# Three passes over the experts' weights: token operands of passes 2 and 3 made in pass 1, roundings one product later, weight differences beside the raw weights

## The chip, the cores and the metric

The kernel runs on one core of one Trainium2 chip. The metric is the device time of one execution in microseconds (us); three runs of the kernel before gave 2467.0, 2466.58 and 2462.47, median 2466.58. Durations come from one profiled execution of that kernel, which took 2462.07 us.

## What is computed

The reference has three parts, one behind the other (cut to what matters):

```
scores = q k^T / 8; keep those >= rowmax - tau; attn = softmax(scores) v       # 4 batches, 8 heads, 576 tokens, 64 wide
x = attn as 2304 x 512
x = (silu(x w_gate) * (x w_val)) w_out                                         # 512 -> 1536 -> 512
logits = x w_gate2; P = exp(logits - max); 8 rounds of row and column scaling  # 2304 x 8 gates
out = sum over e of 8:  P[:, e] * (max(x w1[e], 0) w2[e])                      # 512 -> 1024 -> 512, all in float32
```

The change lies in the last part, the eight experts, which every token passes.

## The kernel before

**Tiling.** Tokens lie in 6 blocks of 384 (`BLK`). The experts' part runs in three passes, each over two blocks (u = 0, 1, 2) and in each over all weights in 32 steps k (`NG`): 8 experts by 4 pairs of 128 hidden units. A matmul operand is kept as two fp32r tiles, the rounded value ("hi") and the rest ("lo"), and a product is three matmuls: hi by hi, hi by lo, lo by hi. Making the two is called a rounding here: ScalarE (ACT) copies to fp32r, then GpSimd (POOL) or VectorE (DVE) subtracts.

**Seven products.** A 2 x 2 block product is done with 7 block products and additional sums on both sides, in the order `UP_ORDER = (1, 2, 6, 5, 7, 4, 3)`. So a step needs seven token operands X (`x_op`, L1019: blocks 11, 21, 22 and four differences t1 to t4) and seven weight operands. One product is 6 matmuls of 384 columns. Product 2 adds to a copy of product 1 (`copy_act(b, a)` in `up` and `up_gated`, on ACT).

**Pass 1 (u = 0, loop at L1619).** Each step loads w1 and w2 raw, makes the weight operands (`a_steps` for the next step's first layer, `b_steps` for this step's second layer, `t_steps` for the differences of the second layer), and stores them to DRAM (`a_store`, `b_store`, `t_store`) for the later passes. `up(k, 0)` gives the seven products; between them `between(n)` runs one sixth of `mix(k - 1)` (6 matmuls `y` of 512 columns, the second layer of the step before, added up by DVE at L1382) and n entries of `w_parts`, the list of pieces of weight work. Entries go to the engines' queues in the order in which the list is emptied. The last step also makes the X of pass 2 (`x_first`, `x_second`, `x_sums`).

**Passes 2 and 3.** `up_gated` fetches the stored weight operands through `a_in`, and `down_gated` those of the second layer through `b_in` (class `Stream`, three tiles ahead, 768 KB each), for groups of two steps. Between two products of `up` stands one half of a down product (6 matmuls). The hidden values are summed on DVE (L1499 to L1501, L1508) and rounded: `split` puts the rounding into the list `later`, which `finish` empties right behind each product, before the next half of a down product. DVE adds the down results into `sums` (L1540). When pass 2 ends, `turn_out(1)` writes its output and `x_rest(2)` makes the X of pass 3.

**What sets the order.** The schedule is manual: each engine, and SyncE's DMA queue (SP), works in the order of the program text. Tiles come from 26 slots of 6 KB a partition: `new` takes the slot that has been free longest, `drop` gives one back, and the next user waits until the last reader (a store, too) is done. A tag of a pool with `bufs=2` (`cv` holds the raw w2 of a step and, in passes 2 and 3, the gates `p`) makes its third tile wait in the same way for all readers of the first.

Of the kernel before, what the change touches and what calls it, by code (L numbers as in the profile page):

```python
# [19 lines left out]
P = 128  # L20
# [111 lines left out]
def attention_moe_moe_kernel(  # L132
# [886 lines left out]
    def x_op(u, nm, x, eng):  # L1019

        t = new([P, 2, 2, BLK], F32R, f"X{u}_{nm}")
        xo[u, nm] = hi, lo = t[:, 0], t[:, 1]
        copy_act(hi, x)
        eng.tensor_tensor(lo, x, hi.bitcast(F32), op=ALU.subtract)
# [32 lines left out]
    x_kept = {i: dram.tile([P, CC, BLK], F32, tag=f"kx{i}", name=f"kx{i}") for i in range(4, NBLK)}  # L1057
    p_kept = dram.tile([1, E * NT], F32, tag="kp", name="kp")
# [64 lines left out]
    def b_steps(k):  # L1123
# [4 lines left out]
    wt = {}  # L1128

    def t_steps(k):  # L1130

        f1, f2 = raws.pop(("b", k))
        t1, t3, t4, t2 = f2[:, 0], f2[:, 1], f1[:, 0], f1[:, 1]

        def one():
            nc.vector.tensor_tensor(t1, f2[:, 1], t1, op=ALU.subtract)
            nc.vector.tensor_tensor(t3, f1[:, 1], t3, op=ALU.subtract)

        def two():
            nc.vector.tensor_tensor(t2, t2, t1, op=ALU.subtract)  # L1140
            nc.vector.tensor_tensor(t4, t4, t2, op=ALU.subtract)

        wt[k] = [new([P, 2, 2, DM // 2], F32R, f"t{k}_{n}") for n in range(2)]
        yield one
        yield two
        yield from b_split(wt[k][1], f2, nc.gpsimd)
        yield from b_split(wt[k][0], f1, nc.vector)
# [129 lines left out]
    def up(k, u):  # L1277
# [4 lines left out]
        def mm(ps, n, start):  # L1282
            a, b = a_of(k, n), xo[u, PARTS[n]]
# [147 lines left out]
    def up_gated(u, k):  # L1431
# [7 lines left out]
        def mm(ps, n, start):  # L1439
            y = 7 * x + UP_ORDER.index(n)  # L1440
            a = a_in.unit(u, g, y).rearrange("p (a d f) -> p a d f", a=2, d=2)
            bh, bl = xo[u, PARTS[n]]
# [72 lines left out]
    def add7(n, m):  # L1515
        nc.vector.tensor_tensor(sums7[n], sums7[n], sums7[m], op=ALU.add)
# [3 lines left out]
    def down_gated(u, g):  # L1520


        for j, n in enumerate(DOWN_ORDER):
# [13 lines left out]
            if g == 0:  # L1537
                copy_act(sums7[n], t[:, :, 0:BLK])
            else:
                nc.vector.tensor_tensor(sums7[n], t[:, :, 0:BLK], sums7[n], op=ALU.add)  # L1540
            if g == NG // GROUP - 1:
                for x in LAST.get(n, ()):
                    later.append(lambda x=x: add7(*x))
            yield

    def turn_out(u):

        for x in range(0, 2 * NTB, 2):
            t = ps_d.tile([P, 2, 512], F32, tag="d", name=f"t{u}_{x}")
            for y in range(2):  # L1550
                half, n = divmod(x + y, NTB)
                for d in range(CC):
                    src = sums7[((4, 7), (2, 3))[half][d // 2]][:, d % 2, n * P:(n + 1) * P]
                    nc.tensor.transpose(t[:, y, d * P:(d + 1) * P], src, ident)
# [13 lines left out]
    def x_rest(u):  # L1568

        (b11, b21), (b12, b22) = ((x[:, 0:2, :], x[:, 2:4, :]) for x in x2[2 * u:2 * u + 2])  # L1570

        def less(out, a, b):
            return lambda: nc.vector.tensor_tensor(out, a, b, op=ALU.subtract)

        def op(nm, x, eng):
            return lambda: x_op(u, nm, x, eng)

        yield op("11", b11, nc.gpsimd)
        yield op("21", b21, nc.gpsimd)
        yield less(b11, b12, b11)  # L1580
        yield op("22", b22, nc.gpsimd)
        yield less(b12, b22, b12)
        yield less(b22, b22, b11)
        yield op("t2", b22, nc.vector)
        yield op("t1", b11, nc.gpsimd)
        yield op("t3", b12, nc.vector)
        yield less(b21, b21, b22)
        yield op("t4", b21, nc.vector)

        def done():  # L1590
            drop(f"x2_{2 * u}")
            drop(f"x2_{2 * u + 1}")

        yield done

# [22 lines left out]

    for k in range(NG):  # L1619
# [3 lines left out]
        if k:  # L1623
            b_store(k - 1)
            w_parts.extend(t_steps(k - 1))
# [7 lines left out]

        next(products)
        between(3)
        next(products)
        next(products)
        between(3)
        w_some(max(0, len(w_parts)))
        if k + 1 < NG:  # L1640
            w_parts.extend(a_steps(k + 1))
        b_load(k)
        if k:
            t_store(k - 1)
        next(products)
        between(2)
        next(products)
        between(3)
        next(products)
        between(3)  # L1650
        next(products)
        w_parts.extend(b_steps(k))
        a_drop(k)
        if k == NG - 1:
            for nm in ("11", "21", "22", "t1", "t2", "t3", "t4"):
                drop(f"X0_{nm}")
            w_some(99)
            w_parts.extend(x_sums(1))
            w_some(2)
        between(2)  # L1660
        w_some(2 if k == NG - 1 else 99)
        if k == NG - 4:
            x_first(1)
        if k == NG - 3:
            x_second(1)
# [11 lines left out]
        if k == 1:  # L1677
            logits_t(5)
            sink = gate_steps()

    b_store(NG - 1)
    fill = mix(NG - 1, 0)
    later.extend(t_steps(NG - 1))
    later.append(lambda: t_store(NG - 1))
    later.append(lambda: gates_load(1, 0))

    def finish():
        n = len(later)
# [3 lines left out]
    def drop_x(u, n):  # L1692
        drop(f"X{u}_{PARTS[n]}")

    between(3)
    between(3)
    w_some(99)
    finish()
    for _ in range(7):
        free_slot = new([P, 2, 2, BLK], F32R, f"halves{len(free_halves)}")  # L1700
        free_halves.extend(free_slot[:, n] for n in range(2))
    products = up_gated(1, 0)
    for n in range(7):
        next(products)
        if n in (0, 2):
            between(0)
        finish()
    products = up_gated(1, 1)
    for n in range(7):
        next(products)  # L1710
        if n in (0, 2):
            between(0)
        finish()
# [7 lines left out]
    for x in range(4):  # L1721
        free_slot = new([P, 2, 2, BLK], F32, f"sums{x}")
        for n in range(2):
            sums7[2 * x + n + 1] = free_slot[:, n]
    b_in.begin()

    x_parts = iter(())
    downs = iter(())

    def slots14(u, g):  # L1730
        nonlocal x_parts
        last = u == 1 and g == NG // GROUP - 1
        for x in range(GROUP):
            k = GROUP * g + x
            if k % PAIRS == PAIRS - 1 and k + 1 < NG:
                gates_load(u, k // PAIRS + 1)
            if last and x == 0:
                x_load(2)
                x_parts = x_rest(2)
            products = up_gated(u, k)  # L1740
            for n in UP_ORDER:
                next(products)
                if last and x == GROUP - 1:
                    drop_x(u, n)
                    next(x_parts, lambda: 0)()
                finish()
                next(downs, None)

    for g in range(1, NG // GROUP):
        downs = down_gated(1, g - 1)  # L1750
        slots14(1, g)

    gates_load(2, 0)
    downs = down_gated(1, NG // GROUP - 1)
    for n in range(7):
        next(downs)
        finish()
        next(x_parts, lambda: 0)()
    for fn in x_parts:
        fn()  # L1760
    products = up_gated(2, 0)
    for n in UP_ORDER:
        next(products)
        finish()
        next(downs)
    for _ in downs:
        pass
    outs = turn_out(1)
    products = up_gated(2, 1)
    for n in range(7):  # L1770
        next(products)
        finish()
        if n in (0, 2, 4):
            next(outs)
    for _ in outs:
        pass
    for g in range(1, NG // GROUP):
        downs = down_gated(2, g - 1)
        slots14(2, g)
    downs = down_gated(2, NG // GROUP - 1)  # L1780
    outs = turn_out(2)
    for n in range(14):
        next(downs)
        finish()
        if n == 11:
            next(outs)
# [36 lines left out]
```

## Time and profile before

| | us |
|---|---|
| median of three runs | 2466.58 |
| profiled execution | 2462.07 |
| its span, first to last instruction | 2460.3 |
| attention and the middle part | 0 to 780 |
| pass 1 | about 780 to 1381 |
| boundary of passes 1 and 2 | 1381 to 1446 |
| passes 2 and 3, with their boundary at 1892 to 1990 | 1446 to 2424 |
| end | 2424 to 2460 |
| mean granted TensorE clock, share of 2.4 GHz | 0.988 |

A matmul is pipelined, so its duration (334 ns for 384 columns) is about twice the distance between two starts; time that TensorE (PE) lost is read from the starts. Idle times in brackets stand before an instruction, with what ended them.

### The profile page before, as it was taken

The numbers are of one execution on the slowest core, as the hardware profiler recorded it, in microseconds if no ns is written. First come the engines' busy times: TensorE is split into PE (matmuls) and PEld (weight loads), VectorE is DVE, ScalarE is ACT, GpSimd is POOL, SyncE is SP. The second block draws the span as 40 slices with busy tenths as digits, with TensorE's granted clock in tenths as the row PEclk, the third lists the DMA queues.
The fourth block names the chain that finished last, engine by engine and source line by source line (L and its number), as shares of the span: only waits on it lengthen the run. The fifth ranks groups of instructions, "written<-read, shape, count | busy, mean of one in ns | idle before, by whom it ended". The sixth has DMA issues, their size and how long they took to land.

```text
span 2460.3 us, 35124 instructions
## 1 busy us (share of the span) xinstructions
PE 2279.4 (93%) x12787; PEld 2083.2 (85%) x12787; DVE 1684.4 (68%) x2735; ACT 971.1 (39%) x1847; POOL 1132.4 (46%) x1074
## 2 busy tenths in 40 slices
PE   7999989999999999899999889999999899999997
PEld 6777779999998777777777689999998799999997
DVE  6999975667542587666666657777777767777775
ACT  4777753322232443443444333333333333333332
POOL 4888755455453444444445433333334233333331
PEclk9999999999999999999999999999999899999999
DMA  8666621111100766677777577777777677777773
GB/s 208 153 162 159 140 85 41 39 39 39 39 18 1 259 256 231 252 261 277 261 278 274 208 266 236 244 239 243 238 244 243 213 235 240 237 242 239 244 236 115
DMA packets 210349, 469.54 MB, mean 191 GB/s; under 512 B 56048, under 2 KB 102272, under 8 KB 210176
## 3 DMA queue, kind: packets, MB, share of 16 engines
q1 hardware_dynamic: 210176, 467.30, 58.0%
q8 instruction: 101, 1.65, 0.3%
q14 instruction: 72, 0.59, 0.1%
HBM read 311.71 MB, written 126.16 MB: 178 GB/s over the span
## 4 chain that ended last, share of the span: by engine, by line
PE 55%; DVE 19%; POOL 7%; issue 7%; ACT 6%; DMA 3%; SPq 1%; ACTq 0%; POOLq 0%; DVEq 0%
PE d L844 5%; PE d L846 5%; PE d L845 5%; PE up L1444 4%; PE up L1446 4%; PE up L1445 4%; DVE s L1499 3%; PE up L1286 2%; PE y L845 2%; DVE s L1508 2%; PE up L1288 2%; PE up L1287 2%; PE y L846 2%; PE v L844 2%; PE v L846 2%
## 5 line engine op out<-in xcount | busy, mean ns | idle before, releaser
L1540 DVE TENSOR_TENSOR sums<-d,sums 128x768 f32<-128x768 f32 x210 | 199.4, 950 | 161.2 <-PE d L846 161.2
L1467 POOL TENSOR_TENSOR halves<-s,halves 128x384 fp32r<-128x384 f32 x192 | 244.8, 1302 | 66.7 <-ACT halves L194 66.7
L1467 POOL TENSOR_TENSOR h<-u,h 128x384 fp32r<-128x384 f32 x64 | 66.3, 1036 | 397.4 <-PE up L1446 199.9
L844 PE MATMUL d<-halves,B 128*128 128x384 f32 x640 | 215.0, 336 | 0.0
L845 PE MATMUL d<-halves,B 128*128 128x384 f32 x640 | 214.6, 335 | 0.0
L846 PE MATMUL d<-halves,B 128*128 128x384 f32 x640 | 214.5, 335 | 0.0
L1444 PE MATMUL up<-X,A 128*128 128x384 f32 x384 | 136.1, 354 | 66.8 <-ACT up L194 66.8
L194 ACT ACTIVATE halves<-s 128x384 fp32r<-128x384 f32 x256 | 134.2, 525 | 134.9 <-DVE s L1499 96.7
L845 PE MATMUL y<-b,h 128*128 128x512 f32 x384 | 159.8, 416 | 26.5 <-POOL b L1121 26.5
L989 POOL TENSOR_TENSOR h<-av,h 128x384 fp32r<-128x384 f32 x72 | 88.7, 1233 | 198.1 <-ACT h L194 198.1
L1444 PE MATMUL up<-X_t,A 128*128 128x384 f32 x512 | 172.8, 337 | 4.7 <-ACT av L194 3.1
L1446 PE MATMUL up<-X_t,A 128*128 128x384 f32 x512 | 172.2, 336 | 0.0
L1445 PE MATMUL up<-X_t,A 128*128 128x384 f32 x512 | 172.2, 336 | 0.0
L1382 DVE SCALAR_TENSOR_TENSOR acc<-y,gate_p,acc 128x512 f32<-128x512 f32 x144 | 107.3, 745 | 94.3 <-PE y L846 93.7
L844 PE MATMUL y<-b,h 128*128 128x512 f32 x384 | 151.4, 394 | 4.9 <-ACT b L194 4.9
L846 PE MATMUL y<-b,h 128*128 128x512 f32 x384 | 153.6, 400 | 0.0
L1467 POOL TENSOR_TENSOR h<-s,h 128x384 fp32r<-128x384 f32 x64 | 65.7, 1026 | 185.9 <-ACT h L194 185.9
L1444 PEld LDWEIGHTS up<-X,A 128*128 128x128 f32 x384 | 72.7, 189 | 87.0 <-ACT up L194 86.8
L478 DVE SCALAR_TENSOR_TENSOR em<-ns,st,ee 128x576 f32<-128x576 f32 x144 | 138.1, 959 | 10.0 <-POOL st L465 7.6
L985 DVE TENSOR_TENSOR av<-v,s 128x384 f32<-128x384 f32 x72 | 40.0, 556 | 153.2 <-PE v L846 137.8
L194 ACT ACTIVATE u<-up 128x384 f32<-128x384 f32 x96 | 46.7, 486 | 221.8 <-PE up L1446 217.3
L1082 POOL TENSOR_TENSOR wa<-a,wa 128x768 fp32r<-128x768 f32 x32 | 59.1, 1848 | 162.1 <-ACT wa L194 142.4
(598 smaller groups left out, 7215.0 us busy)
## 6 DMA issues: line engine op xcount, KB each, us to landing
A<-ka SPq DMA_DIRECT2D x128, 768.0 KB, 4.3
B<-kb SPq DMA_DIRECT2D x128, 768.0 KB, 6.5
kb<-t SPq DMA_DIRECT2D x64, 512.0 KB, 5.0
ka<-wa SPq DMA_DIRECT2D x32, 768.0 KB, 4.5
ka<-wb SPq DMA_DIRECT2D x32, 768.0 KB, 5.9
kk<-khl SPq DMA_DIRECT2D x64, 320.0 KB, 5.4
b<-in_moe_w_dram SPq DMA_DIRECT2D x64, 256.0 KB, 4.4
kb<-b SPq DMA_DIRECT2D x32, 512.0 KB, 6.3
```

The source lines that it names most:

```text
L194: nc.scalar.activation(out=o, in_=i, func=AF.Copy)
L478: nc.vector.scalar_tensor_tensor(m, sc.pop(t), stat.pop(t)[:, 1:2], ee.pop(t), op0=ALU.is_le, op1=ALU.mult, accum_out=sums[p][:, s:s + 1],)
L844: nc.tensor.matmul(ps, a[0], b[0], start=start, stop=False)
L845: nc.tensor.matmul(ps, a[0], b[1], start=False, stop=False)
L846: nc.tensor.matmul(ps, a[1], b[0], start=False, stop=stop)
L989: nc.gpsimd.tensor_tensor(h[:, 1], av, h[:, 0].bitcast(F32), op=ALU.subtract)
L1382: nc.vector.scalar_tensor_tensor(a, t, gate_p[:, i * NTB + n, e:e + 1], a, op0=ALU.mult, op1=ALU.add)
L1444: nc.tensor.matmul(ps, a[:, 0, d], bh[:, d], start=start and d == 0, stop=False, skip_group_check=True)
L1445: nc.tensor.matmul(ps, a[:, 0, d], bl[:, d], start=False, stop=False, skip_group_check=True)
L1446: nc.tensor.matmul(ps, a[:, 1, d], bh[:, d], start=False, stop=d == 1, skip_group_check=True)
L1467: eng.tensor_tensor(h[:, 1], src, h[:, 0].bitcast(F32), op=ALU.subtract)
L1540: nc.vector.tensor_tensor(sums7[n], t[:, :, 0:BLK], sums7[n], op=ALU.add)
```

## The change

The token operands of passes 2 and 3 are made during pass 1, two pieces at the end of each step from k = 10 on (`x_make`), and stored to DRAM; in the last step of the pass before, `x_fetch` loads one behind each product into a slot. `split`'s entries are run behind the next product (`slot`, `settle`), not behind their own. In pass 1 the raw w2 is loaded at the start of the step; its differences are written into the lo halves of the tiles `t` in which they will be rounded, at the end of the same step, and rounded in the next step behind the products 7 and 4. The weight work gets another order. The gates of pass 2 are asked for at the start of the last step of pass 1. `sums` gets an eighth tile, and pass 2's output is written in the first steps of pass 3 in which down products already run.

```diff
     def b_steps(k):
+        raw = raws.pop(("b", k))
         wb[k] = [new([P, 2, 2, DM // 2], F32R, f"b{k}_{n}") for n in range(2)]
-        for o, t in zip(wb[k], raws["b", k]):
+        for o, t in zip(wb[k], raw):
             yield from b_split(o, t, nc.gpsimd)
+        wt[k] = [new([P, 2, 2, DM // 2], F32R, f"t{k}_{n}") for n in range(2)]
+        (b21, b22), (b11, b12) = ((t[:, 0], t[:, 1]) for t in raw)
+        (t4, t2), (t1, t3) = ((t[:, 0, 1].bitcast(F32), t[:, 1, 1].bitcast(F32)) for t in wt[k])
         def one():
-            nc.vector.tensor_tensor(t1, f2[:, 1], t1, op=ALU.subtract)
-            nc.vector.tensor_tensor(t3, f1[:, 1], t3, op=ALU.subtract)
+            nc.vector.tensor_tensor(t1, b12, b11, op=ALU.subtract)
+            nc.vector.tensor_tensor(t3, b22, b12, op=ALU.subtract)
...
+    def t_steps(k):
+        for n, eng in ((1, nc.gpsimd), (0, nc.vector)):
+            yield from b_split(wt[k][n], wt[k][n][:, :, 1].bitcast(F32), eng)
...
+    def x_make(u):
+        if u == 2:
+            yield lambda: x_load(u)
...
+        def keep():
+            nm = box.pop("nm", None)
+            if nm is not None:
+                kept = xo_kept[u, nm] = dram.tile([P, 4 * BLK], F32, tag=f"kx{u}{nm}", name=f"kx{u}{nm}")
+                hi = xo.pop((u, nm))[2]
+                nc.sync.dma_start(kept, hi.bitcast(F32).rearrange("p a d n -> p (a d n)"))
+                drop(f"X{u}_{nm}")
...
+    def x_fetch(u, n):
+        nm = PARTS[n]
+        drop(f"X{u - 1}_{nm}")
+        t = new([P, 2, 2, BLK], F32R, f"X{u}_{nm}")
+        xo[u, nm] = t[:, 0], t[:, 1]
+        nc.sync.dma_start(t.bitcast(F32).rearrange("p a d n -> p (a d n)"), xo_kept[u, nm])
...
     for k in range(NG):
...
         if k:
             b_store(k - 1)
-            w_parts.extend(t_steps(k - 1))
+        b_load(k)
         products = up(k, 0)
...
         if k == NG - 1:
             a_in.begin()
+            gates_load(1, 0)
...
+        for n in UP_ORDER:
+            next(products)
+            if k == NG - 1:
+                x_fetch(1, n)
+            if n == 7 and k:
+                w_parts.extend(t_steps(k - 1))
+            if n == 4:
+                w_some(99)
+                if k:
+                    t_store(k - 1)
+                w_parts.extend(b_steps(k))
+            if n != 2:
+                between(3 if n == 7 else 2)
         a_drop(k)
...
+        w_some(99)
+        if k > 2 * PAIRS + 1:
+            next(x_parts, lambda: 0)()
+            next(x_parts, lambda: 0)()
...
+    def settle(n):
+        for _ in range(n):
             later.popleft()()
...
+    def slot(products):
+        n = len(later)
+        next(products)
+        settle(n)
...
+            for y, n in enumerate(UP_ORDER):
+                slot(products)
+                if u < PASSES - 1 and k == NG - 1:
+                    x_fetch(u + 1, n)
+                if x == 0 and y in (0, 2, 4):
+                    next(outs, None)
+                next(downs)
```

## Rows read from the trace of the kernel before

**Rows 1.** The page: span, and TensorE's busy time, share and instructions.

```profile
span 2460.3 us, 35124 instructions
PE 2279.4 (93%) x12787; PEld 2083.2 (85%) x12787; DVE 1684.4 (68%) x2735; ACT 971.1 (39%) x1847; POOL 1132.4 (46%) x1074
```

**Rows 2.** Windows by stage: length, then busy us (instructions) per engine, clock, DMA share, GB/s.

```profile
480.00:540.00 60.00, 60.00 (x348) 60.00 (x347) 47.51 (x52) 16.64 (x27) 33.80 (x19) 1.00 0.17 53
...
1014.00:1381.00 367.00, 343.86 (x1631) 289.49 (x1631) 236.28 (x437) 148.16 (x293) 174.19 (x126) 1.00 0.75 274
1381.00:1446.00 65.00, 48.89 (x218) 43.93 (x216) 39.35 (x54) 21.57 (x41) 26.21 (x19) 0.87 0.62 221
1446.00:1892.00 446.00, 417.62 (x2362) 408.69 (x2363) 315.03 (x434) 144.19 (x288) 166.09 (x143) 1.00 0.71 237
1892.00:1990.00 98.00, 82.42 (x452) 80.51 (x451) 68.45 (x86) 37.28 (x67) 38.31 (x30) 0.93 0.69 239
1990.00:2424.00 434.00, 408.18 (x2312) 399.55 (x2311) 306.47 (x424) 135.97 (x273) 158.08 (x136) 1.00 0.71 237
```

**Rows 3.** Waits of TensorE, whole span: us in total, times, longest.

```profile
PE up L1444 <- ACT up L194: 66.8, 62, 3.5
PE y L845 <- POOL b L1121: 26.5, 63, 1.6
PE up L1286 <- ACT u L194: 14.1, 29, 1.4
```

**Rows 4.** Timeline of TensorE in one step of pass 1: start, duration, instruction, idle.

```profile
1136.40 0.40 PE L844 MATMUL y<-b,h 128*128 128x512 f32 x1
1137.20 0.50 PE L845 MATMUL y<-b,h 128*128 128x512 f32 x1 [0.40 <-POOL b L1121]
1137.54 0.40 PE L846 MATMUL y<-b,h 128*128 128x512 f32 x1
1137.77 0.40 PE L844 MATMUL y<-b,h 128*128 128x512 f32 x1
1138.44 0.51 PE L845 MATMUL y<-b,h 128*128 128x512 f32 x1 [0.27 <-POOL b L1121]
...
1147.12 0.40 PE L846 MATMUL y<-b,h 128*128 128x512 f32 x1
1147.97 0.44 PE L1286 MATMUL up<-X_t,wb 128*128 128x384 f32 x1 [0.46 <-ACT u L194]
```

**Rows 5.** Timeline of ScalarE in the same step.

```profile
1146.69 0.84 ACT L194 ACTIVATE wa<-a 128x768 fp32r<-128x768 f32 x1 [4.00 <-DVE a L1086]
1147.45 0.47 ACT L194 ACTIVATE u<-up 128x384 f32<-128x384 f32 x1
...
1152.75 1.15 ACT L194 ACTIVATE b<-b 128x512 fp32r<-128x512 f32 x2
```

**Rows 6.** Timeline of one step of pass 2, lines of VectorE, ScalarE and TensorE.

```profile
1694.86 1.40 DVE L1499 TENSOR_TENSOR s<-s,s 128x384 f32<-128x384 f32 x1
1696.29 0.56 DVE L1500 TENSOR_TENSOR s<-s,u 128x384 f32<-128x384 f32 x1
...
1699.03 0.34 PE L846 MATMUL d<-halves,B 128*128 128x384 f32 x1
...
1699.83 0.52 ACT L194 ACTIVATE halves<-s 128x384 fp32r<-128x384 f32 x1 [0.49 <-DVE s L1508]
1700.26 0.47 ACT L194 ACTIVATE up<-up 128x384 f32<-128x384 f32 x1
...
1700.78 0.44 PE L1444 MATMUL up<-X,A 128*128 128x384 f32 x1 [1.41 <-ACT up L194]
```

**Rows 7.** A window at the boundary of passes 1 and 2, columns as in rows 2.

```profile
1425.00:1430.00 5.00, 2.19 (x7) 2.23 (x8) 2.56 (x4) 1.51 (x4) 1.71 (x2) 0.60 1.01 412
```

**Rows 8.** DMA issues: count, KB each, median us to landing.

```profile
kb<-t SPq DMA_DIRECT2D x64, 512.0 KB, 5.0
x<-kx SPq DMA_DIRECT2D x2, 768.0 KB, 6.1
```

More of the change, by code (lines that the diff above doesn't have):

```diff
@@ L1 @@
+import itertools
 import math
@@ L1566, in x_load, with less, fn, op @@
             nc.sync.dma_start(x2[i], x_kept[i])
[L1568 to L1588, printed above, removed]
+    def x_make(u):
+        if u == 2:
+            yield lambda: x_load(u)
+        box = {}
+        def less(n, m, o):
+            def fn():
+                y = box["y"]
+                nc.vector.tensor_tensor(y[n], y[m], y[o], op=ALU.subtract)
+            return fn
+        def keep():
[5 more added lines that the diff above has]
+                drop(f"X{u}_{nm}")
+        def op(nm, n, eng):
+            def fn():
+                keep()
+                if "y" not in box:
+                    box["y"] = [x[:, y:y + 2] for x in x2[2 * u:2 * u + 2] for y in (0, 2)]
+                x_op(u, nm, box["y"][n], eng)
+                box["nm"] = nm
+            return fn
+        yield op("11", 0, nc.gpsimd)
+        yield op("21", 1, nc.gpsimd)
+        yield less(0, 2, 0)
+        yield op("22", 3, nc.gpsimd)
+        yield less(2, 3, 2)
+        yield less(3, 3, 0)
+        yield op("t2", 3, nc.vector)
+        yield op("t1", 0, nc.gpsimd)
+        yield op("t3", 2, nc.vector)
+        yield less(1, 1, 3)
+        yield op("t4", 1, nc.vector)
         def done():
+            keep()
             drop(f"x2_{2 * u}")
@@ L1679, in attention_moe_moe_kernel @@
             sink = gate_steps()
+    for fn in x_parts:
+        fn()
     b_store(NG - 1)
-    fill = mix(NG - 1, 0)
     later.extend(t_steps(NG - 1))
     later.append(lambda: t_store(NG - 1))
-    later.append(lambda: gates_load(1, 0))
-    def finish():
-        n = len(later)
+    def settle(n):
         for _ in range(n):
             later.popleft()()
[L1692 to L1698, printed above, removed]
-    for _ in range(7):
[L1700 to L1713, printed above, removed]
+    def slot(products):
+        n = len(later)
+        next(products)
+        settle(n)
+    for _ in range(7):
+        t = new([P, 2, 2, BLK], F32R, f"halves{len(free_halves)}")
+        free_halves.extend(t[:, n] for n in range(2))
+    fill = mix(NG - 1, 0)
+    for k in range(GROUP):
+        products = up_gated(1, k)
+        for n in UP_ORDER:
+            slot(products)
+            if n in (1, 7, 3):
+                next(fill)
+        if k == 0:
+            b_in.begin()
     for _ in fill:
@@ L1720, in attention_moe_moe_kernel @@
     ps_d = ctx.enter_context(tc.tile_pool(name="ps_d", bufs=2, space=PSUM, reuse_waits="tile"))
[L1721 to L1732, printed above, removed]
+    t = [new([P, 2, 2, BLK], F32, f"sums{x}") for x in range(4)]
+    sums7.update((n, t[n // 2][:, n % 2]) for n in range(8))
@@ L1733, in slots14 @@
+    groups = [(u, g) for u in range(1, PASSES) for g in range(NG // GROUP)]
+    outs = iter(())
+    for (u, g), (u0, g0) in zip(groups[1:], groups):
+        downs = down_gated(u0, g0)
         for x in range(GROUP):
             k = GROUP * g + x
[L1735 to L1739, printed above, removed]
-            products = up_gated(u, k)
[L1741 to L1755, printed above, removed]
-        next(downs)
[L1757 to L1784, printed above, removed]
+            if (k + 1) % PAIRS == 0:
+                u1, e1 = divmod((u * NG + k + 1) // PAIRS, E)
+                if u1 < PASSES:
+                    gates_load(u1, e1)
@@ new lines, in attention_moe_moe_kernel @@
+            products = up_gated(u, k)
+            for y, n in enumerate(UP_ORDER):
+                slot(products)
+                if u < PASSES - 1 and k == NG - 1:
[3 more added lines that the diff above has]
+                next(downs)
+        for _ in downs:
+            pass
+        if g0 == NG // GROUP - 1:
+            outs = turn_out(u0)
+    downs = down_gated(*groups[-1])
+    outs = turn_out(PASSES - 1)
@@ L1785, in attention_moe_moe_kernel @@
+    for n in range(14):
+        m = len(later)
+        next(downs)
+        settle(m)
         if n == 11:
+            settle(len(later))
             next(outs)
```

64 lines of the change are left out of this document (17 added, 47 removed).

## The prediction

> **What bounds the kernel now.** I read the page first: TensorE (PE) is 93% busy [rows 1], which says little, since a matmul's duration covers two starts. So I took the windows by stage. From 480 to 540 us nothing makes PE wait: 348 matmuls of 384 columns in 60 us, 0.1724 us each [rows 2]. That is the pace to which every later stage is held. From 1446 to 1892 there are 2362 such matmuls, 407.2 us at that pace, in 446 us; from 1990 to 2424 there are 2312, 398.6 us, in 434 us [rows 2]. Passes 2 and 3 thus lose 38.8 and 35.4 us in their steady parts, though VectorE (DVE) is busy for only 315 of 446 us there. The boundary of the two passes has 452 matmuls in 98 us, 24 of them small transposes: about 76 us of work, 22 lost. The boundary of passes 1 and 2 has 218 in 65 us, some 48 of them with 512 columns, about 40 us of work, 25 lost, at a mean clock of 0.87 [rows 2].
>
> The waits of PE say what for: 66.8 us in 62 waits of a product for ScalarE's (ACT) copy `up`, 26.5 us in 63 waits of `y` for GpSimd's (POOL) lo half of `b`, 14.1 us in 29 waits for ACT's copy `u` [rows 3]. That is one wait a step in passes 2 and 3, and two and one a step in pass 1. The idle times understate the loss, because the pipeline drains first; the starts give it all.
>
> **Pass 1, step by step.** The distance of starts behind a 512-column matmul is 0.23 us (1137.54 to 1137.77). The first wait for `b` takes 0.80 us from start to start (1136.40 to 1137.20), so it costs 0.57, and the next start comes 0.11 late (0.34); the second costs 0.44 and again 0.11; that for `u` 0.62 and 0.11 [rows 4]. Together 1.96 us a step. A check: 367 us hold 1631 matmuls, 20.9 steps of 78, so a step takes 17.55 us; 42 x 0.1724 + 36 x 0.231 = 15.56, and 15.56 + 1.96 = 17.52.
>
> Why they are late: both copies of `b` start at 1152.75, behind the last product, and the copy `u` stands on ACT behind the copy `wa` of 0.84 us, which itself had waited for DVE [rows 5]. With the new list the first half of `b` is rounded behind product 4, one product and one `mix` (2.4 us) earlier, and the second no longer stands behind the first on POOL; `wa` and `wb` are copied before product 5, so that ACT is free for `u`. The raw w2 is asked for at the start of the step and needed some 12 us later; a 512 KB store lands in 5.0 us [rows 8], so that cover is wide. All three waits should go: 30 steps x 1.96 = **-59 us**. What would be late next is the second lo half of `b`, by my placing of the durations 0.8 us before its use.
>
> What pass 1 pays. (a) 25 of the 26 slots are in use in steps 5 to 9, while `second` lives: 7 X, 2 blocks of x, 6 weight tiles `w`, 4 `b`, 2 `t`, 4 sums. Then the second new `t` gets the slot of the `t` just stored, and DVE's differences at the end of the step wait for a store that is issued 1 to 2 us before and lands after 5.0 us [rows 8]. DVE stands for about 3.5 us, behind it the sums for the next `wa`, ACT's copies, product 7: 1.3 us a step by that chain, **+6**, between 0 and 15 (later steps have two or more spare slots). (b) The operands for passes 2 and 3 are the same 14 copies and 14 subtractions as before, only moved; new are 14 stores of 768 KB here. An ACT copy of this shape takes 0.84 us [rows 5] at the end of the step, where the next product's copy has about as much room. In step 16 the load of x is followed at once by the copy that needs it: landing 6.1 us [rows 8], ACT stands in order, **+7**. Stores that wait for POOL hold up SP, and with it the loads of w2, in perhaps five steps: **+5**. For (b) between 0 and 21.
>
> **Boundary of passes 1 and 2: not what the diff suggests.** The X work there goes (its 25 us), but `gates_load(1, 0)` now stands at the start of step 31, and its tile shares the two buffers of `cv` with that step's raw w2, whose last readers are DVE's differences at the end of the step. SP works in order, so all seven fetches of X stand behind it. DVE reaches those differences about 2.7 us after product 1 of pass 2 would be due. Then come gates (384 KB), X 11 and so on. The queue has moved 412 GB/s when full [rows 7], 1.9 us for 768 KB; the first fetch lands about 5 us after its issue [rows 8], 8 us late, the last, behind two stores of `t`, at about 22 us, where product 3 would be due at about 9. PE loses about 13 us, and 2 more since the clock falls in such idle stretches (0.60 in that window, between the levels 1.2 and 2.4 GHz [rows 7]). **-25 + 15 = -10**, between -22 (a fetch that is not held) and 0. The Trainium skill (DMA: Bandwidth & Descriptors, Where 436 GB/s comes from) has HBM at about 358 GB/s as the limit of a core; by that a fetch takes 2.2 us and this boundary 2 us more. The trace does not agree, with 412 over 5 us [rows 7].
>
> **Passes 2 and 3.** At 1699.03 the down half ends, at 1700.78 product 2 starts: 1.75 us instead of 0.17. It waits for the copy at 1700.26, which stands on ACT behind the rounding of the last sum (1699.83), which waits for DVE's L1508 [rows 6]. With `settle` that rounding comes behind the copy in ACT's order. Product 1, which the copy reads, stands one down half ahead (6 x 0.1724 = 1.03 us), and the copy takes 0.47: with the drain, done some 0.3 us before product 2 is due. The roundings themselves, one product later, are needed first by a down product several products on. The 57 steady waits cost by starts what the windows show, 74 us, some 70 of it this wait. I leave 3: **-67**. POOL and DVE get no new work.
>
> **Boundary of passes 2 and 3.** 22 us now, mostly X made in place. After: 7 fetches (5.5 MB) beside 3.6 MB of weights in one step, 9.1 MB, 22 us at 412 GB/s against 14.5 us; the streams run three tiles ahead, so I expect 1 to 2 us, and as much for output transposes that share two down buffers: **-22 + 5 = -17**. The **end** has no fewer waits: 0.
>
> **Sum:** -59 + 18 - 10 - 67 - 17 = -135 against the profiled execution's 2462.07 us (2460.3 of span and 1.8 around it): **2327**. The median of the runs shown is 4.5 higher, within their spread; I keep 2327.
>
> **Rivals.**
> - *The copy stays late in passes 2 and 3.* L1499 takes 1.40 us and L1500 behind it, of the same shape, 0.56 [rows 6]. If POOL's roundings come to stretch L1500 and L1501 likewise (by 0.84 each), ACT's third rounding of a sum, still ahead of the copy, ends 1.7 us later, and product 2 waits about 0.8 us a step: 60 x 0.75 = 45, **2372**. For: 1.40 is there. Against: POOL's three roundings of the sums can begin only behind ACT's first, when L1500 is nearly over. The Trainium skill (SBUF — State Buffer, Who interferes with whom) has it that a DVE instruction with two SBUF inputs stands fully behind a GpSimd one that reads SBUF; by that rule this rival would be certain. In part the trace agrees (1.40 against 0.56).
> - *Pass 1 keeps its step time,* since DVE's tail (differences, x sums) makes ACT late elsewhere: -59 + 18 falls away, **2368**. Against: DVE is busy for 236 of 367 us.
> - *The fetch is not held* and the first boundary is hidden as the second: **2315**.
> - *Slower than before:* the store of `t` becomes a loop through pass 1. If it lands in some 10 us rather than 5.0, and in all 31 steps, DVE stands until 9 us into the next step; PE then idles 4 us a step, and a clock of 0.6 for 5 us costs 2.5 more: 31 x 6.5 = 201, **2529**. It decides from 4.3 us a step on (135 / 31). Against it: spare slots outside steps 5 to 9.
>
> **How the numbers follow.** Forecast (2300 to 2350) 0.55; late copy 0.16; pass 1 unchanged 0.15; fetch not held 0.08; slower 0.04; 0.02 for gains and losses that cancel. Low end: 18 and 11 us of costs gone and 7 more of waits, 2327 - 36 = 2291. High end: late copy and double cost in pass 1, 2327 + 45 + 18 = 2390. A measurement tells 0.2%, 5 us, from no change: faster 0.94, same 0.02, slower 0.04.
>
> **What would show it.** Right: windows of pass 1 with 78 matmuls in about 15.6 us, of passes 2 and 3 with 84 in 14.5; no wait of PE for `up` and hardly one for `b`; on SP in step 31 a long gap ahead of `p`, the seven fetches close together behind it, and TensorE waiting for DMA of X at the first boundary alone; one wait near step 17 for a copy behind x's load. Wrong: PE still waiting for ACT `up` in each step; DVE's differences standing for DMA in most steps; waits of `d` for B.

## The result, and the profile after

The changed kernel takes **2349.52 us** (median of 4 runs, 2347.02 to 2350.73) beside 2464.53 for the kernel before: a ratio of 0.9532, 95% interval 0.9515 to 0.9548. The profiled execution is that of 2347.02 us; against the one of before (2462.07) it is 115 us shorter, where 135 were forecast. The time is 1% above the forecast of 2327 and just inside its range of 2300 to 2350: 0.5 us below the upper end, with one of the four runs above it.

The page of the kernel after, its span and TensorE's line, as in [rows 1]:

```profile
span 2345.2 us, 35095 instructions
PE 2247.5 (96%) x12787; PEld 2087.9 (89%) x12787; DVE 1681.2 (72%) x2736; ACT 968.0 (41%) x1847; POOL 1133.7 (48%) x1073
```

As many matmuls and all but the same work on the others. The busy time of TensorE again says little; its windows say more (columns as in [rows 2]):

```profile
1140.00:1200.00 60.00, 50.77 (x233) 43.30 (x232) 44.36 (x73) 24.50 (x46) 27.51 (x20) 0.94 0.90 321
1260.00:1320.00 60.00, 60.00 (x300) 53.82 (x300) 44.57 (x81) 26.67 (x51) 32.05 (x23) 1.00 0.87 303
1355.00:1380.00 25.00, 14.61 (x62) 12.89 (x61) 10.40 (x18) 5.76 (x12) 6.14 (x6) 0.80 0.92 359
1380.00:1400.00 20.00, 15.08 (x73) 13.36 (x72) 11.10 (x18) 5.08 (x11) 8.51 (x8) 0.95 1.03 406
1440.00:1500.00 60.00, 60.00 (x348) 60.00 (x347) 45.10 (x66) 20.07 (x41) 23.49 (x20) 1.00 0.75 255
```

Pass 2 (1440 to 1500) holds 348 matmuls in 60 us: it is at the pace of the undisturbed stage at 480 [rows 2], which has not changed (348 here too). So is a step of pass 1 in which nothing but the weights is prepared (1260 to 1320: 300 matmuls, where [rows 2] had 1631 in 367 us, 267 in 60). But a step of pass 1 in which operands X are made as well (1140 to 1200) has only 233, fewer than before, and the first boundary (1355 to 1400) is slow still.

TensorE's waits over the whole span, the larger ones of the passes (us in total, times, longest):

```profile
PE up L1289 <- ACT up L195: 12.4, 10, 2.9
PE up L1447 <- DMA X<-kx: 10.4, 2, 8.3
PE y L846 <- POOL b L1124: 8.3, 19, 1.0
PE up L1447 <- DMA A<-ka: 4.9, 2, 3.6
PE d L845 <- DVE sums L1546: 3.9, 3, 3.3
PE y L845 <- ACT b L195: 3.8, 3, 2.0
```

The 66.8 us in 62 waits for `up` in passes 2 and 3 [rows 3] are down to 0.8 us in 2; `b` costs 8.3 us in place of 26.5. New are ten waits of pass 1's products for ACT's copy `up` (L1289), and two for X at the first boundary.

Since waits understate a loss, I add up the starts: each start of TensorE less the one before it and less the pace of the earlier instruction (0.1724 us for 384 columns, 0.231 for 512, a fixed allowance for narrower ones). Pass 1 is counted from 780 us to 60 us ahead of the last `y`, the first boundary from there to 25 us behind that `y`, the second from 30 us ahead of the first output transpose to 60 us behind it.

| loss of TensorE, us | before | after | measured | forecast |
|---|---|---|---|---|
| pass 1 | 83.6 | 57.7 | -26 | -41 |
| boundary of passes 1 and 2 | 27.5 | 21.0 | -6.5 | -10 |
| passes 2 and 3 | 75.0 | 4.9 | -70 | -67 |
| boundary of passes 2 and 3 | 23.1 | 10.3 | -13 | -17 |
| end | 11.4 | 8.3 | -3 | 0 |
| ahead of 780 us (untouched) | 177.7 | 180.9 | +3 | 0 |

The sum is -115, the difference of the two executions. Over all runs of this study the untouched first stage lies between 177.7 and 182.7: 5 us of scatter that no change explains, so single profiles are compared stage by stage and not by their ends.

Two places need explaining: 15 us won too little in pass 1, and what keeps the first boundary at 21 us.

**A step of pass 1 that makes X.** ScalarE (first fence), VectorE (second) and TensorE (third), timeline of the end of such a step (start, duration, engine, line, instruction, in brackets the idle time ahead of it and its releaser):

```profile
1156.48 0.84 ACT L195 ACTIVATE X_t<-x 128x768 fp32r<-128x768 f32 x1 [4.42 <-DVE x L1584]
1157.23 0.47 ACT L195 ACTIVATE up<-up 128x384 f32<-128x384 f32 x1
```

```profile
1153.42 0.98 DVE L1138 TENSOR_TENSOR t<-b 128x256 f32<-128x256 f32 x1
...
1155.44 0.95 DVE L1584 TENSOR_TENSOR x<-x,x 128x768 f32<-128x768 f32 x1
```

```profile
1157.75 0.44 PE L1289 MATMUL up<-X,wa 128*128 128x384 f32 x1 [2.85 <-ACT up L195]
```

ACT rounds an X whose input `less` (L1584) makes on DVE in the same step, and there `less` stands behind the four weight differences (L1138 to L1143). ACT works in order, so it stands 4.42 us, and the copy `up` of the next product 1 stands behind the X: TensorE starts product 2 at 1157.75, 3.0 us late. Two of the ten waits for the copy `up` have this cause. By the starts five of the ten cost more than 1.5 us: these two 3.0 each; one behind the load of x, 2.2; one in which the roundings of X stood for the store of a `t`, whose slot they take, 2.2; and one for that and for DVE's differences, 1.8. The other trouble of such steps is on SP. Its queue, issues and what it waited for between 985 and 1245 us:

```profile
1077.83 4.90 SPq L1592 DMA_DIRECT2D kx1t<-X_t  x2
...
1089.52 2.35 SPq L1120 DMA_DIRECT2D b<-in_moe_w_dram  x2
```

```profile
SPq L1592 <- DVE X_t L1026: 6.7, 2, 3.6
...
SPq L1592 <- POOL X L1026: 3.9, 1, 3.9
SPq L1592 <- POOL X_t L1026: 3.8, 1, 3.8
```

With two roundings a step, the store of the first (L1592) is issued right as the second begins, and waits for the first one's lo half: 14.4 us in four waits. Behind it stand the loads of raw w2 (L1120), which `b` then lacks; they land 6.6 us after their issue in these steps and 6.0 in the plain ones, so it is mostly the issue that is late (the second load of a step goes out 10.9 us behind the step's first matmul in steps 11 to 23, and 7.9 in steps 24 to 29, both medians).

### The profile page after: what moved, and what is told of

It reads as the page before. It is cut to its first block, busy times and chain, and to the rows that moved or that the text cites. A ratio compares the mean times of both kernels' runs of the same rounds, so it can differ in the third digit from the quotient of the medians.

```text
span 2345.2 us, 35095 instructions
## 1 busy us (share of the span) xinstructions
PE 2247.5 (96%) x12787; PEld 2087.9 (89%) x12787; DVE 1681.2 (72%) x2736; ACT 968.0 (41%) x1847; POOL 1133.7 (48%) x1073
## 4 chain that ended last, share of the span: by engine, by line
PE 76%; DVE 8%; POOL 5%; DMA 4%; issue 3%; ACT 2%; SPq 1%; ACTq 0%; POOLq 0%; DVEq 0%
PE d L845 8%; PE d L847 8%; PE d L846 8%; PE up L1447 6%; PE up L1449 6%; PE up L1448 6%; PE y L846 2%; PE up L1289 2%; PE y L847 2%; PE y L845 2%; PE up L1290 2%; PE up L1291 2%; PE v L845 2%; PE v L846 2%; PE v L847 2%
## 5 line engine op out<-in xcount | busy, mean ns | idle before, releaser
L1470 POOL TENSOR_TENSOR halves<-s,halves 128x384 fp32r<-128x384 f32 x192 | 245.7, 1306 | 67.4 <-ACT halves L195 67.4
L1470 POOL TENSOR_TENSOR h<-u,h 128x384 fp32r<-128x384 f32 x64 | 65.7, 1026 | 309.2 <-ACT h L195 155.6
L1470 POOL TENSOR_TENSOR h<-s,h 128x384 fp32r<-128x384 f32 x64 | 64.7, 1011 | 196.1 <-ACT h L195 107.5
L1447 PE MATMUL up<-X,A 128*128 128x384 f32 x384 | 130.4, 340 | 16.1 <-DMA X<-kx 10.4
L1448 PE MATMUL up<-X,A 128*128 128x384 f32 x384 | 129.6, 338 | 0.0
L1449 PE MATMUL up<-X,A 128*128 128x384 f32 x384 | 129.6, 337 | 0.0
```

The source lines that it names most:

```text
L1470: eng.tensor_tensor(h[:, 1], src, h[:, 0].bitcast(F32), op=ALU.subtract)
```

## The experiments

Twelve kernels, told in the order of the questions. All ratios are against the kernel before.

**Passes 2 and 3: is it the put-off rounding?**

```
 def slot(products):
-    n = len(later)
     next(products)
-    settle(n)
+    settle(len(later))
```

> The changed kernel with one thing undone: in passes 2 and 3 every rounding is issued right behind the product that made its input, not one product later. Theory (the prediction's): PE's wait for ACT's copy up comes back in every step, 1.2 us from start to start in some 60 steps, about 70 us, so 2350 + 70 = 2420 us (2405 to 2430), with 60 waits for up at L1447 to L1449 and 84 matmuls in about 15.6 us. Rival: passes 2 and 3 came to pace through the rest of the change (operands fetched, streams begun otherwise); then 2350 to 2360 and no such waits.

Measured 2421.42 us (2419.29 to 2422.64; 0.9824 [0.9808, 0.9840]): +71.9. The waits of TensorE in that run, and a window of pass 2 as above:

```profile
PE up L1447 <- ACT up L195: 57.8, 59, 1.7
```

```profile
1440.00:1500.00 60.00, 56.23 (x320) 54.95 (x319) 43.70 (x61) 18.93 (x38) 22.30 (x19) 1.00 0.72 245
```

The wait is back in every step, 59 times, and by the starts passes 2 and 3 lose 72.7 us, where the kernel before lost 75.0. The theory holds with its size; what else the change did moved these passes by some 2 us.

**Pass 1: which half of the list brought what?** First `b` late, then `a` late:

```
             if n == 4:
                 w_some(99)
                 if k:
                     t_store(k - 1)
+            if n == 3:
                 w_parts.extend(b_steps(k))
```

> The changed kernel with one thing undone in pass 1: the list of b (rounding of w2, then the differences) is begun behind the last product of a step again, not behind product 4. Theory (the prediction's): the two waits of y for POOL's lo half come back, 1.23 us a step by the starts, 30 steps, 37 us, less the few that are there now: 2350 + 33 = 2383 us (2375 to 2395); with the differences in the same place in DVE's order. Rival: the list's place does not matter once the copies wa and wb stand earlier: 2350 to 2358.

Measured 2361.60 us (2359.16 to 2365.42; 0.9586 [0.9570, 0.9601]): +12, not +33.

```
+        if k:
+            w_parts.extend(t_steps(k - 1))
         for n in UP_ORDER:
...
+            if n == 6:
+                w_some(99)
+                if k + 1 < NG:
+                    w_parts.extend(a_steps(k + 1))
+                if k:
+                    t_store(k - 1)
```

(the places that the change gave to the three lists of `a`, `t` and the store are taken out)

> The changed kernel with the other half of pass 1's list undone: the list of t at the start of a step and that of a behind product 6, as before; the list of b stays behind product 4. Theory (the prediction's): the wait of product 7 for ACT's copy u behind the copy wa comes back, 0.73 us a step from the starts, 30 steps: 22 us; and since the run with b late cost only 12 us of the 37 worked out, part of the waits of y may have been the copy wc standing ahead of b on ACT, so up to 16 us more: 2349 + 30 = 2379 us (2368 to 2390). Rival: with b early, ACT has room again and the place of a does not matter: 2349 to 2357.

Measured 2382.57 us (2381.47 to 2384.76; 0.9664 [0.9649, 0.9678]): +33. The waits of the run with `b` late, then of that with `a` late:

```profile
PE y L846 <- POOL b L1124: 18.5, 37, 1.2
```

```profile
PE y L846 <- POOL b L1124: 17.8, 54, 1.0
PE up L1289 <- ACT u L195: 14.4, 28, 1.3
```

`y` waits for `b` in both. With `a` late the reason is seen on POOL and ACT, at the end of a step of that run:

```profile
1288.55 0.42 ACT L195 ACTIVATE wc<-a 128x256 fp32r<-128x256 f32 x1 [1.87 <-DVE a L1095]
1288.87 1.14 ACT L195 ACTIVATE b<-b 128x512 fp32r<-128x512 f32 x2
```

```profile
1289.04 0.74 POOL L1085 TENSOR_TENSOR wc<-a,wc 128x256 fp32r<-128x256 f32 x1 [0.81 <-ACT wc L195]
1289.74 2.52 POOL L1124 TENSOR_TENSOR b<-b,b 128x512 fp32r<-128x512 f32 x2
```

The last piece of `a`, `wc`, waits 1.87 us for DVE, and `b` stands behind it on ACT and again on POOL, although it was in its new place in the list. The same row stands in the trace of the kernel before: `wc` stands on ACT at 1152.05, after 1.87 us idle for DVE, ahead of the `b` of [rows 5]. So part of the wait that I had put down to the place of `b` came from `a` being late. Together the two runs give back 45 us of the 59; both halves undone in one kernel was not tried.

**Pass 1: what does making X cost?** First the kernel with X apart:

```
-        yield op("21", 1, nc.gpsimd)
-        yield less(0, 2, 0)
-        yield op("22", 3, nc.gpsimd)
-        yield less(2, 3, 2)
+        yield both(op("21", 1, nc.gpsimd), less(0, 2, 0))
+        yield both(op("22", 3, nc.gpsimd), less(2, 3, 2))
...
-        yield op("t3", 2, nc.vector)
-        yield less(1, 1, 3)
+        yield both(op("t3", 2, nc.vector), less(1, 1, 3))
...
             next(x_parts, lambda: 0)()
-            next(x_parts, lambda: 0)()
```

> The changed kernel with the making of X spread over steps 10 to 27 in place of 10 to 22: one rounding a step, each subtraction of blocks behind that step's rounding and so a step ahead of the rounding that needs it, and the load of x in a step of its own, one step ahead of its use. Nothing is left out. Theory: what pass 1 lost above the forecast is ACT standing in order, with the copy of the next product 1 behind it, for a rounding of X whose input DVE makes behind the weight differences, or x's load; the waits of 2 to 3 us at the head of five steps go: 2350 - 12 = 2338 us (2333 to 2341). Rival: the loss is SP's, whose stores of X wait for the lo halves and make the loads of w2 late; the stores are as many here, so only the 2.2 us behind the load of x go: 2345 to 2349, with the waits of y for b still there.

Measured **2330.00 us** (2328.11 to 2332.38; 0.9456 [0.9442, 0.9471]): -19.5, more than I expected. Pass 1 loses 41.8 us in place of 57.7, and the waits for product 1's copy are small; that of ACT for the raw w2 (second fence, 985 to 1245 us) is not:

```profile
PE up L1289 <- ACT up L195: 5.4, 8, 1.0
```

```profile
ACT b L195 <- DMA b<-in_moe_w_dram: 17.1, 11, 4.4
```

The stores, as many as before, now follow a step behind their rounding, and SP no longer waits for lo halves: L1592 is gone from its waits. It also makes one X a step in place of two. So this kernel changes several things at once: ACT's order, SP's waits and the load of a step. Two more runs take one of them each. The load of x alone, moved one step ahead:

```
-        if u == 2:
-            yield lambda: x_load(u)
...
             drop(f"x2_{2 * u + 1}")
+            if u == 1:
+                x_load(2)
```

> The changed kernel with one thing moved: the load of x for pass 3 stands in the step that drops the x of pass 2, one step ahead of its first rounding; by that the pairs of pass 3 are those of pass 2, in which no rounding follows a subtraction that it needs within one step. Two roundings and two stores a step remain, unlike in the run with X apart (2330). Theory 1 (ACT stands in order for DVE): the waits of 3.0, 1.8 and 3.0 us at product 1 and the 2.2 behind the load go: 2349 - 9 = 2340 us (2336 to 2343), the other 10 us of the run with X apart being the transfers. Theory 2 (transfers: two stores of 768 KB a step fill the queue, so w2 and t's slots are late): only the 2.2 behind the load go: 2345 to 2348.

Measured 2340.43 us (2338.86 to 2341.64; 0.9493 [0.9477, 0.9509]): -9.1, as theory 1 had it; the longest wait at product 1 falls from 2.9 to 2.3 us. Not all was won: the load, 1.5 MB ahead of a step's w2, made one copy of `b` later still (6.0 us in one wait of `y`, 2.0 in the changed kernel). And the stores alone:

```
-                kept = xo_kept[u, nm] = dram.tile([P, 4 * BLK], F32, tag=f"kx{u}{nm}", name=f"kx{u}{nm}")
-                hi = xo.pop((u, nm))[2]
-                nc.sync.dma_start(kept, hi.bitcast(F32).rearrange("p a d n -> p (a d n)"))
+                xo_kept[u, nm] = a_kept[len(xo_kept) % 4][:, 0:3]
+                xo.pop((u, nm))
...
```

> The changed kernel (not the one with X apart) with the 14 stores of X left out: the operands are rounded as before, two a step, and dropped; passes 2 and 3 fetch tiles of kept weights of the same size in their place, so that the boundaries move the same bytes. X apart gained 19.5 us, of which moving the load of x alone gave 9. Theory (the other half are transfers: two stores of 768 KB a step fill the queue, w2 and the slots come late): the waits of y behind a late w2 (2.1 + 1.1 and 0.8 + 1.1) and some of the waits at product 1 go: 2349.5 - 8 = 2341 us (2337 to 2344). Rival (all of it is ACT's order): 2347 to 2350.

Measured 2333.31 us (2331.23 to 2334.78; 0.9465 [0.9450, 0.9481]): -16, twice what I expected. By the starts pass 1 loses 46.0 us, 11.7 less. ACT's waits of that run between 985 and 1245 us:

```profile
ACT X_t L195 <- DVE x L1584: 7.5, 2, 3.7
...
ACT b L195 <- DMA b<-in_moe_w_dram: 2.0, 3, 0.9
```

and the second of these in the changed kernel:

```profile
ACT b L195 <- DMA b<-in_moe_w_dram: 19.1, 9, 5.1
```

The wait for `less` stays (8.5 us in 2 waits in the changed kernel), that for w2 all but goes. Both causes are real: the stores some 12 us by the starts, ACT's order and x's load 7 (57.7 - 51.1 by the run with the load early), against 16 with X apart. This run takes SP's wait for the lo half away together with the 11 MB and with the time for which a store holds X's slot, so it doesn't part these. X apart speaks against SP's wait as the whole of it: that wait is gone there, and ACT still lacks w2 for 17.1 us in 11 waits; the second load goes out 9.8 us into a step, at the median of steps 11 to 23, against 10.9 in the changed kernel and 8.3 without the stores. So the transfers themselves make w2 late too. By the starts X apart wins 7.6 of its 16 us at the copy `up` and 3.0 at `y`; the rest is spread over starts without a wait.

**The first boundary: a held fetch, or bytes?** The first try moved gates_load behind the step:

```
             a_in.begin()
-            gates_load(1, 0)
...
+    gates_load(1, 0)
     b_store(NG - 1)
```

> The changed kernel with gates_load(1, 0) moved from the start of step 31 to behind the whole step, so that the seven fetches of X do not stand on SP's queue behind its wait for the two buffers of raw w2. Theory: the first fetch is then issued behind product 1 of step 31 and landed long before pass 2; the 8.5 us at product 1 and the 2.2 us at the next operand go, and most of the half clock behind them: 2350 - 11 = 2339 us (2334 to 2342). Rival: the boundary is bound by bytes (5.5 MB of operands beside stores and streams), so the wait only moves to a later operand or to the A stream: 2346 to 2352, with as many us of PE waiting for DMA.

Measured 2347.70 us (2344.70 to 2348.70; 0.9526 [0.9512, 0.9540]): -1.8, not to be told from no change. It tells less than I wanted. The wait for X falls from 8.3 to 4.7 us, but a wait of 6.7 us for ACT's `u` takes its place: p now lands behind the seven X. The next run shows that chain; it is X apart with gates_load behind the step and three fetches made ahead:

```
+        if NG - 1 > k >= NG - 4:
+            x_fetch(1, UP_ORDER[k - (NG - 4)], drops=False)
...
```

> The kernel with X apart (2330.0), gates_load behind step 31 as in the run before, and three of the seven operands of pass 2 fetched ahead, one at the end of each of steps 28, 29 and 30, into spare slots. Theory: the first boundary is bound by bytes in the queue, 1.9 us for 768 KB; three fetches fewer in the burst take 5.7 us off the wait at product 1 and later, and with the clock behind them 6 to 12 us: 2321 us (2316 to 2325). Rival: it is SP's order (the fetches stand behind the stores of step 31 whatever their number): 2328 to 2332.

Measured 2331.07 us (2328.93 to 2332.73; 0.9453 [0.9439, 0.9467]): no gain on 2330.0. By the starts the boundary loses 4.1 us less and pass 1 6.5 more, as I read it since the early fetches stand ahead of w2 in SP's queue. And p is late, on DVE and then ACT:

```profile
1362.36 0.56 DVE L1459 SCALAR_TENSOR_TENSOR s<-up,p 128x384 f32<-128x384 f32 x1 [9.95 <-DMA p<-kp]
```

```profile
1363.01 0.52 ACT L195 ACTIVATE h<-s 128x384 fp32r<-128x384 f32 x1 [10.23 <-DVE s L1459]
1363.43 0.47 ACT L195 ACTIVATE u<-up 128x384 f32<-128x384 f32 x1
```

So p must stay ahead of X and yet not be held. In a spare slot it is neither late nor held:

```
+        if (u, e) == (1, 0):
+            t = gates[u, e] = new([P, 2 * BLK], F32, "p1_0")
...
```

> The kernel with X apart (2330.0) with gates_load(1, 0) where the change has it, at the start of step 31, but its tile in a spare slot in place of the buffers of raw w2: it is not held, and neither are the fetches of X behind it. (In the run with gates_load behind the step, p landed behind all of X, DVE stood 10 us for it, ACT's rounding behind that, and PE lost 6.3 to 6.9 us at product 7; so that run took one hold away and made another.) Theory (the hold): the 8.7 us at product 1 and 2.3 at the next operand go but for some 3 to 5 us of queue: 2330 - 7 = 2323 us (2319 to 2326). Rival (bytes): the queue is full from step 31 on anyway, so what is won at X is lost at later operands and the A stream: 2327 to 2332.

Measured 2326.20 us (2324.72 to 2330.70; 0.9433 [0.9421, 0.9446]): 3.8 below the kernel with X apart, their ranges overlapping; by the starts the boundary loses 19.2 in place of 20.8. The hold is worth 2 to 4 us at most, although it was there: SP's wait ahead of `p` in the changed kernel is

```profile
SPq L1432 <- DVE t L1139: 4.7, 1, 4.7
```

In the changed kernel the first fetch is issued at 1358.70 and lands 6.1 us later; with the hold gone it takes 11.1 us (1333.89 to 1345.00), and pass 2 still waits 6.5 us for it. Then two fetches ahead, behind w2 this time:

```
                     t_store(k - 1)
+                if NG - 1 > k >= NG - 3:
+                    x_fetch(1, UP_ORDER[k - (NG - 3)], drops=False)
...
```

> The same as the run with p in a slot, and two operands of pass 2 fetched ahead, one each in steps 29 and 30, behind that step's loads of w2 and stores of t in SP's queue (not ahead of the loads of w2, as in the run with three early, where pass 1 lost 6 us by it). Theory (bytes in the burst): two fetches of 1.9 us fewer, 4 us less than the run with p in a slot. Rival: the queue has no room in steps 29 and 30 either and pass 1 pays it back: the same time within 2 us.

Measured 2326.76 us (2322.95 to 2328.35; 0.9431 [0.9418, 0.9444]): the same time; the boundary loses 3.2 us less, pass 1 2.1 more. And three fetches left out:

```
+        if n in UP_ORDER[:3]:
+            if u == 1:
+                xo[u, nm] = xo[0, nm]
+                return
...
```

> The same as the run with p in a slot, but the fetches of the first three operands of pass 2 are left out (its products 1, 2 and 6 read those of pass 1, still in place), so 2.3 MB of the burst are not moved; everything else is done. Theory (bytes): 3 x 1.9 = 5.7 us and some clock less than the run with p in a slot: 6 to 9 us. Rival (the hold was all): within 2 us of it.

Measured 2320.15 us (2318.50 to 2323.17; 0.9408 [0.9395, 0.9421]): -6.05, and by the starts the boundary loses 13.0 in place of 19.2. So it is the fetches themselves and not their place. The window of the run with p in a slot, and that of this run:

```profile
1340.00:1355.00 15.00, 9.81 (x41) 8.88 (x42) 4.03 (x8) 2.92 (x6) 2.30 (x2) 0.77 1.00 406
```

```profile
1340.00:1355.00 15.00, 13.20 (x60) 11.53 (x58) 7.91 (x15) 4.44 (x9) 5.14 (x4) 0.89 0.99 395
```

The DMA engines are busy all the time at 406 GB/s, TensorE waits and its clock is granted at 0.77 of full speed, a mean between its two levels, 1.2 and 2.4 GHz. With 2.3 MB fewer it runs 60 matmuls in place of 41, at a granted clock of 0.89. Bytes and the number of transfers were not parted.

**The second boundary.** The run with p in a slot, with the output transposes two products later:

```
-                if x == 0 and y in (0, 2, 4):
+                if x == 0 and y in (2, 4, 6):
```

> The kernel with X apart and p in a slot (2326.2), with the three output transposes of pass 2 issued behind products 6, 7 and 3 of the next step in place of 1, 6 and 7. Theory (second boundary): the 3.5 us that a down product waits for a buffer, one held by the transposes' copy and one by DVE's sum behind a queue of additions, go for the most part: 2326 - 3 = 2323 us (2320 to 2325). Rival: DVE's queue of additions is what is late, and the wait only moves: 2325 to 2328.

Measured **2321.39 us** (2320.17 to 2324.47; 0.9421 [0.9407, 0.9435]), the best kernel of the study that does all the work. This boundary loses 4.7 us in place of 9.1. What stood there in the run with p in a slot, on DVE and then on ACT:

```profile
1849.83 1.75 DVE L1525 TENSOR_TENSOR sums<-sums,sums 128x768 f32<-128x768 f32 x1
...
1852.78 0.94 DVE L1549 TENSOR_TENSOR sums<-d,sums 128x768 f32<-128x768 f32 x1
```

```profile
1853.38 1.01 ACT L195 ACTIVATE out<-t 128x1024 f32<-128x1024 f32 x1
```

One of the two down buffers waited for L1549 in DVE's queue, the other, taken by the transposes, for ACT's copy; the next down product started at 1853.78.

## Why the prediction was right, point by point

The mechanisms held where most of the time was won, in passes 2 and 3 and in the plain steps of pass 1. That the total is inside the range is in part luck: in pass 1 one term was missed by 26 us, and others came out 11 better.

- **The three waits of pass 1, -59.** Right in the step: the plain steps at 1260 us hold 300 matmuls in 60 us. Not gone everywhere: by the starts `y` still loses 16 us to late halves of `b` in the other steps, 6 of it ahead of 985 us, where no X is made. Wrong in its shares: I gave 1.23 us a step to the place of `b` and 0.73 to that of `a`, and undoing them singly costs 12 and 33 us. I had followed `b` on ACT, but not the `wc` ahead of it there, which waits for DVE.
- **(a) the slot of the stored `t`, +6.** Too much: DVE's differences waited once, 1.2 us. Copies of X took such slots instead: ACT waited 9.1 us in 8 waits for `kb<-t`, behind which I had nothing.
- **(b) making X, +12, between 0 and 21.** This is the term that was mis-sized. Pass 1 loses 57.7 us where the forecast left 83.6 - 41 = 42.6: 19 of them ahead of 985 us, 38 from 985 to 1245, where X is made, and under 1 in the plain steps from there to 1340. So by the measure of the plain steps making X cost some 38 us and not 12, and the rest of the pass was 11 better than forecast. From 985 to 1245 the kernel with X apart loses 17, and 5 behind, where it still makes X. Named and real were x's load (product 1 late by 2.2 us, and w2 behind it) and SP held by stores (I said 5 us; 12 by the run without them, their transfers and slots among it). Not seen was that ACT's rounding of X waits for DVE's `less` (8.5 us in 2 waits), behind the differences that the same change moves to the end of the step. I had written that the copy at the end of the step finds "about as much room"; it does not where its input is made in the same step.
- **First boundary, -25 + 15.** The first wait came as worked out (8 us forecast, 8.3 measured), so the step looked right, and its cause was not: with the hold taken away only 2 to 4 us go. What counts are the fetches themselves, 5.5 MB in a queue that is full anyway: three of the seven left out take 6.2 of the boundary's 19.2 us, so all seven would be 14, an estimate in proportion. The waits for the A stream behind them (4.9 us) were not foreseen. By the same runs the rival "fetch not held" was priced too high: 12 us.
- **Passes 2 and 3, -67.** Right: -70 in the starts, +71.9 when undone. The margin was as thin as I said (0.3 us behind the copy): in the step at 1600 us the copy ends at 1606.08, and product 2 starts at 1606.45.
- **The late copy as a rival.** It did not come, but the stretching on which it rested is there. One step of pass 2, DVE and POOL:

```profile
1602.80 0.77 DVE L1502 TENSOR_TENSOR s<-s,s 128x384 f32<-128x384 f32 x1
1603.60 0.56 DVE L1503 TENSOR_TENSOR s<-s,u 128x384 f32<-128x384 f32 x1
1604.19 0.56 DVE L1504 TENSOR_TENSOR s<-s,s 128x384 f32<-128x384 f32 x1
...
1607.31 1.37 DVE L1470 TENSOR_TENSOR halves<-s,halves 128x384 fp32r<-128x384 f32 x1
```

```profile
1602.13 1.03 POOL L1470 TENSOR_TENSOR h<-u,h 128x384 fp32r<-128x384 f32 x1 [4.87 <-PE up L1449]
1604.26 3.99 POOL L1470 TENSOR_TENSOR halves<-s,halves 128x384 fp32r<-128x384 f32 x3 [1.11 <-ACT halves L195]
```

  L1502 and the L1470 shown, whose shortest take 0.56 and 0.54 us (of 64 each), end 0.41 us behind POOL's `h` (1603.16) and 0.43 behind its third `halves` (1608.25); as I read it they stood for POOL. The Trainium skill (SBUF — State Buffer, Who interferes with whom) calls the shared ports an exclusive lock, and these rows agree. L1504, the last input of a rounding ahead of the copy, starts before POOL's roundings do, which was the argument against this rival; L1503 and L1504 have medians of 0.56 us over the 64 of each, not the 1.40 that the rival needed.
- **Second boundary, -17.** -13: the streams held (no wait for X there), and the shared down buffers cost 4.4 us (the last run) where I gave them 1 to 2.
- **The other rivals.** Pass 1 did not keep its step time (a plain step takes 15.6 us, 17.55 before), though the matmuls from 985 to 1245 are as few as before (1113, and 1125 before): there DVE's tail did make ACT late, in part as that rival had it. For "slower", DVE's differences would have had to stand for the store of `t`; they did so once. Its price has a slip: 5 us at a clock of 0.6 lose 2.0 us, not 2.5.
- **The end, 0:** -3.

## What to carry to other kernels

Put work off by one product where its result isn't due yet: the order on a shared engine was worth 70 us here, and nothing was computed faster. When pieces are moved to the end of a step, look on each engine for what else was moved there: a rounding belongs a step behind the subtraction that feeds it. That a store belongs a step behind the rounding fits, but was not run by itself. A queue that runs full between two stages is hardly relieved by issuing earlier; moving less shortens it.

## What the runs showed of the hardware

- SP never has more than eight transfers under way in this program. In all 14 traces the count of issued and not yet landed transfers reaches 8 and never 9, and SP then waits for landings that its transfer has nothing to do with: in the run with p in a slot a fetch is issued at 1337.69, when the transfer eight before it has landed at 1337.63. Whether the limit is the chip's or the program's these runs don't show. SP's waits in the run with p in a slot, 1330 to 1365 us:

```profile
SPq L1159 <- DMA X_t<-kx1t: 1.5, 1, 1.5
SPq L1342 <- DMA X_t<-kx1t: 1.5, 1, 1.5
```

  A store of weights and an output store wait for fetches of X. So a burst delays also the issue of what stands behind it.
- With 256 to 768 KB a transfer the queue moved 406 GB/s over 15 us and 414 over 10 (1345 to 1355 in the run with three early). The Trainium skill (DMA: Bandwidth & Descriptors, Where 436 GB/s comes from) puts the limit of a core at about 358 from HBM; these windows are above it.
- A subtraction of 256 columns on DVE takes between 0.41 and 2.06 us (L1139, 32 of them, median 0.41), though its operands are the same in all.
